# Frequency rows of a convolution stored with the channel block last, and the first MLP weights split earlier

## The chip, the cores and the metric

The kernel runs on one core of a Trainium2 chip. The metric is the device time of one execution in microseconds, median over runs; lower is better. PE is the matrix engine, ACT, DVE and POOL the scalar, vector and GpSimd engines, SP the engine that issues most transfers. `S.dma_start` issues a transfer from ACT, `nc.gpsimd.dma_start` from POOL.

## The reference

A block of 2048 tokens with 640 channels and adaptive layer norms, all in float32:

```
sa, ca, ga, sb, cb, gb = (silu(c) @ w_mod) in six parts of 640
h = layernorm(x) * (1 + ca) + sa
K = real(sum_n C_n B_n dt exp(dt A_n l)),  l = 0..2047          # a state-space kernel per channel
y = irfft(rfft(h, 4096) * rfft(K, 4096))[:2048] + h * Dskip     # long convolution along the tokens
x = x + ga * y
h = layernorm(x) * (1 + cb) + sb
x = x + gb * ((silu(h @ w1) * (h @ w3)) @ w2)                   # w1, w3: 640 x 1728
```

## The kernel before

**The convolution.** The transform is done as matrix products in two stages, of length `NA` = 32 and `NB` = 64. Channels are taken in `NDC` = 5 blocks of `DC` = 128. For each block there are eight groups `g` of four frequencies of the first stage: `stage2(ch, g)` transforms tokens and kernel, `k_copy` (ACT), `products` and `sums` (DVE) multiply them, `inverse1(ch, g)` does the first half of the inverse on PE into PSUM tile `pz`. `z_store` copies `pz` to SBUF tile `zt` on ACT and stores it in the scratch tensor `zs` in HBM: half a channel block (512 KB) at a time for blocks 0 to 3 from SP, and group by group (256 KB) from ACT for block 4 (`z_last`). Each group waits for three-deep buffers of the tables `s2` and `i1`, loaded by SP.

**The way back to tokens.** The second half of the inverse needs all frequencies of a token tile. Tile `j` holds 128 tokens (four values of `b`, 32 of `a`); `z_load(z, j, ks)` loads, for each channel block `k`, 64 partitions (cosine and sine parts of 32 frequencies) of four rows of 128 channels, 128 KB in all. In PE, `i2` turns this into tokens. There are 16 tiles. The first four (`early`, the first 512 tokens) are treated apart, in `x_part(j)`: blocks 0 to 3 come through memory like the others (loaded by POOL, block 3 just before it is used), but for block 4 the last two groups do not make the trip:

- Groups 0 to 5 (`NG` = 6, 24 frequencies) of block 4 are stored, and loaded again as soon as group 5 is stored, two gathers of 48 KB for each tile (cosine and sine rows apart): for tiles 0 to 2 from SP, for tile 3 from ACT. They land in `early[j][1]`, whose rest is zeroed by POOL beforehand. `far_cols` multiplies them with `i2`.
- Groups 6 and 7 are kept: `near_rows(g)` takes 32 columns of `i1` for the 16 values of `b` of the first four tiles, ACT copies the result to `near["z"]`, and `near_cols(g)` multiplies it with tables that `near_tables` built on POOL from the constant `i2d`. `far_cols` adds into the same PSUM tile `pl`.

For the last group, i = 7 of the loop that closes the convolution, PE's order is near_rows(7), `x_part(3)`, near_cols(7), far_cols, the ordinary inverse of group 7, three matmuls `fill`, and after them `keep_warm(IDLE)` with `IDLE` = 7 dummy matmuls. DVE adds `pl` to the 128 channels of each early tile (L1075), takes their statistics (L1078) and aggregates them (L1080).

**The first MLP.** `x_first` makes the power of variance on POOL, two tiles at a time, and normalises the tiles 0 and 2 on ACT and 1 and 3 on DVE. `turn_a` transposes them on PE, and `plain("A", 0, ...)`, the first block of the MLP's weights, begins. All weight products are made from two float32r parts: `split` copies a weight to its high part on ACT (`gh`, `uh`) and subtracts on DVE for the low part (`gl`, `ul`). For block 0 of `wg` and `wu` (`first_w`) the load is issued behind the last load of `i1`, and the split is ordered behind the last product sum of the convolution (`last_sum`). Loads of tiles 4 to 7, of weight block 13 and of weight block 1 follow on SP in the order in which they are written (`SQ`, `sp_order`).

The tile framework orders instructions of an engine by its own plan except where they are kept in program order (`tc.keep_in_program_order`, `ordered`, `acopy`, `act`) or placed behind another (`tc.issue_after`). Pools with `bufs=n` hand out the same n buffers in turn: `rw` (raw weights) has 5, `h` has 18.

Of the kernel before, what the change touches and what calls it, by code (L numbers as in the profile page):

```python
# [9 lines left out]
F32 = mybir.dt.float32  # L10
# [27 lines left out]
def consts():  # L38
# [25 lines left out]
    i2 = np.concatenate([np.cos(ang).T, -np.sin(ang).T] * 2)  # L64
# [17 lines left out]
    i1 = i1.reshape(*i1.shape[:-1], 2, NB).swapaxes(-1, -2).reshape(i1.shape)  # L82
    i2d = np.zeros((4, 16, 2, 2 * NA + 16))
    for fl in range(4):
        for c in range(2):
            for i in range(2):
                i2d[fl, :, c, i * NA:i * NA + NA] = i2[c * NA + (6 + i) * 4 + fl]
            i2d[fl, :, c, 2 * NA:] = np.eye(16)
    i2d = i2d.reshape(P, 2 * NA + 16)
# [27 lines left out]
def tile_kernel(ctx: ExitStack, tc: tile.TileContext, a):  # L117
# [5 lines left out]
    zs = dram.tile([NDC, NB, 2, NA, DC], F32, name="zs")  # L123
# [591 lines left out]
    def inverse1(ch, g):  # L715
# [5 lines left out]
        if ch == NDC - 1 and g >= NG:  # L721
            near_rows(g, i1, Y, pz[:, 0, 2 - 2 * (g % 2), :])
# [9 lines left out]
    near = {}  # L732
# [4 lines left out]
    def near_tables():  # L737

        hc = h_tile()[:, :2 * NA + 16]
        nc.sync.dma_start(hc, a["i2d"])  # L740
        for i in range(8 - NG):
            w = near["w", NG + i] = h_tile()
            G.tensor_tensor(w.rearrange("p (b a) -> p b a", b=16), bc(hc[:, 2 * NA:], 2, NA),
                            bc(hc[:, i * NA:i * NA + NA], 1, 16), op=OP.mult)
        near["z"] = h_tile()
        for x, z, st in early:
            G.memset(z[64:, :, 2 * DC:], 0.0)

    def near_rows(g, i1, Y, pd):
# [44 lines left out]
    def z_last(g):  # L794
# [4 lines left out]
        for j in (range(3), (3,), ())[g - NG + 1] if g >= NG - 1 else ():  # L799
            with tc.issue_after(stored.ins):  # L800
                for c in range(2):
                    r = slice(c * 32, c * 32 + 4 * NG)
                    ins = (S if j == 3 else nc.sync).dma_start(
                        early[j][1][64 + r.start:64 + r.stop, :, 2 * DC:], zsv[r, 4 * j:4 * j + 4, NDC - 1])
# [14 lines left out]
    def h_tile():  # L819
        return xp.tile([P, 512], F32, name="h", bufs=18)  # L820

    def z_tile():
        z = tz.tile([P, SD, 3, NA], F32, name="A")
        return z.rearrange("p k s b -> p (k s b)").rearrange("p (b d) -> p b d", b=4)

    ZW = (2 * DC, 3 * DC)
# [17 lines left out]
    def x_part(j, idle=0):  # L844
# [4 lines left out]
        for b in range(4):  # L849
            for hh in range(2):  # L850
                r, c = slice(hh * 64, hh * 64 + 64), slice(b * NA, b * NA + NA)
                ordered(py[hh][c, :2 * DC], i2[r], z[r, b, :2 * DC], start=True, stop=True,
# [159 lines left out]
    first_w = dict.fromkeys(("wg", "wu"))  # L1012
# [24 lines left out]
    for tk in range(NS - 4, LAG + 8 * NDC + 2):  # L1037
# [17 lines left out]
        if 0 <= i < 8:  # L1055
# [12 lines left out]
            if i == 7:  # L1068
# [3 lines left out]
                x_stats(3)  # L1072
                mv4 = xp.tile([P, 4, 2], F32, name="mv4", bufs=1)
# [37 lines left out]
    IDLE = 7  # L1111
# [21 lines left out]
    def z_place(both):  # L1133
        return wq.tile([P, 2, 2, 512], F32, name=both).rearrange("p a b c -> p (a b c)")[:, :4 * 3 * DC].rearrange(
            "p (b d) -> p b d", b=4)
# [8 lines left out]
    def x_first(tiles, mv):  # L1144
# [9 lines left out]
        for pair, rs in enumerate(powers):  # L1154
            V.scalar_tensor_tensor(rs[:, 2, :], mv[:, 2 * pair:2 * pair + 2, 0], -1.0, rs[:, 1, :],
                                   op0=OP.mult, op1=OP.mult)
            for i in range(2):
# [4 lines left out]
                else:  # L1162
                    V.tensor_scalar(xn, x, mv[:, j, 0:1], rs[:, 1, i:i + 1], op0=OP.subtract, op1=OP.mult)
# [11 lines left out]
    def x_mid(j, got, g):  # L1175
# [3 lines left out]
        for b in range(4):  # L1179
            for hh in range(2):  # L1180
                r, c = slice(hh * 64, hh * 64 + 64), slice(b * NA, b * NA + NA)
                n = ZW[hh]
                PE.matmul(py[hh][c, :n], i2[r], z[r, b, :n], start=True, stop=True, tile_position=(r.start, c.start))
        for hh in range(2):
            h = slice(hh * 256, hh * 256 + ZW[hh])
            V.tensor_tensor(x[:, h], py[hh][:, :ZW[hh]], x[:, h], op=OP.add)
# [97 lines left out]
    ahead = {(0, n): w for n, w in first_w.items()}  # L1284
# [15 lines left out]
    def wk(w, k):  # L1300
        return w[0][:, k, :], w[1][:, k, :]
# [7 lines left out]
    def plain(c, f, h, ws, early=False, between=None, then=None):  # L1309
# [6 lines left out]
        if early and f == 0:  # L1316
            pu = bank(1)
            for lo in range(2):
                for k in range(KD):
                    for ps, ws in ((pg, wgs), (pu, wus)):  # L1320
                        for i in range(1 if lo else 2):
                            end = PE.matmul(ps, ws[i][:, k, :], x[k][lo], start=(k + i + lo == 0),
# [267 lines left out]
    for pair in range(2):  # L1590
# [142 lines left out]
```

## Time and profile before

| | |
|---|---|
| median of 3 runs | 929.12 us (928.58 to 930.3) |
| the profiled execution | 927.25 us |
| its span, first to last instruction | 925.5 us |
| PE busy | 887.9 us, 96% |
| DVE, ACT, POOL busy | 698.9, 548.6, 265.9 us |
| convolution's last group to the MLP's first matmul | about 355 to 374 us |

In the profile's rows, `A<-zs` is a load of a `z` tile (its pool is named A), `zs<-zt` and `zs<-h` are the stores, `pl` is the PSUM tile of near and far columns, `py` that of x_part, `rw` a raw weight, `ps` any PSUM tile of the MLP part. L111 is the line of the helper through which all instructions of the MLP part go. A number in brackets is idle time before the instruction and what ended it. `PEclk` is the granted clock of PE, 1.00 throughout.

### The profile page before, as it was taken

The numbers are of one execution on the slowest core, as the hardware profiler recorded it, in microseconds if no ns is written. First come the engines' busy times: TensorE is split into PE (matmuls) and PEld (weight loads), VectorE is DVE, ScalarE is ACT, GpSimd is POOL, SyncE is SP. The second block draws the span as 40 slices with busy tenths as digits, with TensorE's granted clock in tenths as the row PEclk, the third lists the DMA queues.
The fourth block names the chain that finished last, engine by engine and source line by source line (L and its number), as shares of the span: only waits on it lengthen the run. The fifth ranks groups of instructions, "written<-read, shape, count | busy, mean of one in ns | idle before, by whom it ended". The sixth has DMA issues, their size and how long they took to land.

```text
span 925.5 us, 21047 instructions
## 1 busy us (share of the span) xinstructions
PE 887.9 (96%) x8461; PEld 692.2 (75%) x8461; DVE 698.9 (76%) x1250; ACT 548.6 (59%) x811; POOL 265.9 (29%) x278
## 2 busy tenths in 40 slices
PE   5999889999999998999999999999999999999998
PEld 3776567777777666678888887778888888888886
DVE  6799888999999967876666655686976666664665
ACT  4899899999999743564343323556633333333432
POOL 3633454445446330243222201210522222100000
PEclk9999999999999999999999999999999999999999
DMA  8755898655656887942131217974322211103452
GB/s 254 258 202 192 272 226 216 176 161 157 178 159 174 200 264 213 261 176 86 57 111 60 58 44 217 278 234 153 95 64 71 85 58 57 58 29 100 150 177 101
DMA packets 103765, 140.68 MB, mean 152 GB/s; under 512 B 20212, under 2 KB 62964, under 8 KB 103668
## 3 DMA queue, kind: packets, MB, share of 16 engines
q1 hardware_dynamic: 100108, 129.48, 46.9%
q0 software_dynamic: 2048, 7.34, 2.4%
q10 hardware_dynamic: 1512, 2.52, 0.8%
q8 instruction: 66, 1.08, 0.5%
q14 instruction: 31, 0.25, 0.1%
HBM read 107.85 MB, written 31.46 MB: 151 GB/s over the span
## 4 chain that ended last, share of the span: by engine, by line
PE 67%; ACT 14%; DVE 12%; DMA 4%; issue 2%; SPq 0%; POOL 0%; DVEq 0%; ACTq 0%; POOLq 0%
PE ps L111 58%; ACT A L145 3%; PE p L676 3%; ACT ph L145 2%; ACT cs L145 2%; DVE E L597 2%; ACT L145 2%; DVE uk L111 2%; PE pm L111 1%; DVE A L604 1%; ACT kc L148 1%; PE pt L637 1%; DVE E L600 1%; ACT uk L148 1%; DMA A<-zs 1%
## 5 line engine op out<-in xcount | busy, mean ns | idle before, releaser
L111 DVE TENSOR_TENSOR s<-ps,s 128x512 f32<-128x512 f32 x138 | 95.0, 688 | 80.1 <-PE ps L111 79.8
L570 POOL TENSOR_TENSOR ph<-thi,iota 128x1024 int32<-128x1024 int32 x40 | 86.0, 2150 | 142.3 <-DVE A L608 94.9
L111 DVE TENSOR_TENSOR gl<-rw,gh 128x640 fp32r<-128x640 f32 x87 | 78.1, 897 | 64.3 <-ACT gh L111 64.3
L111 ACT CAST gh<-rw 128x640 fp32r<-128x640 f32 x87 | 63.2, 727 | 100.4 <-PE ps L111 62.6
L111 PE MATMUL ps<-xA,gh 128*128 128x512 f32 x280 | 88.5, 393 | 0.1
L111 PE MATMUL ps<-gh,uh 128*128 128x512 f32 x224 | 87.5, 390 | 0.0
L111 PE MATMUL ps<-gl,uh 128*128 128x512 f32 x224 | 87.2, 389 | 0.0
L111 POOL TENSOR_TENSOR S<-rw 128x256 f32<-128x256 f32 x46 | 36.5, 795 | 174.1 <-DVE S0l L111 163.1
L676 PE MATMUL p<-uk,s 128*64 128x256 f32 x640 | 77.9, 385 | 6.8 <-DVE Y L701 2.4
L111 PE MATMUL ps<-gh,ul 128*128 128x512 f32 x208 | 81.1, 390 | 0.0
L676 PEld LDWEIGHTS p<-uk,s 128*64 128x64 f32 x640 | 44.6, 136 | 29.5 <-DVE Y L701 3.5
L111 PEld LDWEIGHTS ps<-xA,gh 128*128 128x128 f32 x280 | 52.2, 188 | 13.6 <-issue 1.0
L111 PE MATMUL ps<-xA,gl 128*128 128x512 f32 x140 | 54.5, 390 | 0.0
L604 DVE TENSOR_TENSOR A<-A,ph 128x1024 f32<-128x1024 f32 x40 | 51.8, 1295 | 0.0
L111 ACT ACTIVATE s<-ps 128x512 f32<-128x512 f32 (+1 forms) x33 | 19.7, 597 | 53.1 <-PE ps L111 53.1
L597 DVE TENSOR_TENSOR E<-A,cs 128x1024 f32<-128x1024 f32 x40 | 50.2, 1254 | 0.6 <-ACT A L145 0.6
L111 PEld LDWEIGHTS ps<-gl,uh 128*128 128x128 f32 x224 | 42.1, 188 | 9.0
L111 PEld LDWEIGHTS ps<-gh,uh 128*128 128x128 f32 x224 | 42.1, 188 | 8.8
L111 PEld LDWEIGHTS ps<-gh,ul 128*128 128x128 f32 x208 | 39.0, 188 | 8.4
L574 POOL TENSOR_TENSOR ph<-ph,phi 128x512 int32<-128x512 int32 x40 | 44.5, 1115 | 2.5
L727 PE MATMUL pz<-Y,i 64*128 64x128 f32 x640 | 44.4, 278 | 0.7 <-ACT h L148 0.4
L727 PEld LDWEIGHTS pz<-Y,i 64*128 64x128 f32 x640 | 38.9, 187 | 7.1 <-issue 5.8
(251 smaller groups left out, 2287.8 us busy)
## 6 DMA issues: line engine op xcount, KB each, us to landing
rw<-in_w_dram SPq DMA_DIRECT2D x52, 320.0 KB, 2.9
us<-u SPq DMA_DIRECT2D x16, 640.0 KB, 3.2
s<-in_s_dram SPq DMA_DIRECT2D x40, 256.0 KB, 4.8
i<-in_i_dram SPq DMA_DIRECT2D x40, 256.0 KB, 3.3
rw<-in_wg_dram SPq DMA_DIRECT2D x31, 320.0 KB, 3.9
rw<-in_wu_dram SPq DMA_DIRECT2D x28, 320.0 KB, 2.8
uk<-us SPq DMA_DIRECT2D x32, 256.0 KB, 4.6
zs<-zt SPq DMA_DIRECT2D x16, 512.0 KB, 4.8
```

Of the source, the lines that this page charges most:

```text
L111: ins = fn(*args, **kw)
L145: return tc.keep_in_program_order(S.activation(*args, **kw))
L148: return tc.keep_in_program_order(S.copy(out, in_))
L570: keep(G.tensor_tensor(p, bc(thi[:, s * SD:s * SD + SD], 2, NPH), bc(iota, 1, SD), op=OP.mult))
L574: keep(G.tensor_tensor(p[:, :, :NA], p[:, :, :NA], bc(phi[:, s * SD:s * SD + SD], 2, NA), op=OP.add))
L597: keep(V.tensor_tensor(EC[s][:, :, 1:3, :], AA[s][:, :, 1:3, :], mid(cs[s]), op=OP.mult))
L600: keep(V.tensor_tensor(EC[s][:, :, 0, :], AA[s][:, :, 0, :], cs[s][:, :, 2 * NA - 1:NA - 1:-1], op=OP.mult))
L604: keep(V.tensor_tensor(A[:, :, 1:3, :], A[:, :, 1:3, :], mid(ph[s]), op=OP.mult))
L637: keep(PE.matmul(pt[c * 64:c * 64 + 64, g, :], kk[:, g, :], s1[:, c, :], start=True, stop=True, tile_position=(0, c * 64)))
L676: keep(PE.matmul(p2[par * 64:par * 64 + 64, pi, c, :], s2[:, pi * 2 + par, c * 64:c * 64 + 64], uk[:, 0:kn + 1:kn, f, :], start=True, stop ...
L727: ins = keep(PE.matmul(pz[:, par, (g % 2) * 2 + pi, :], i1[r, pi, c, :], Y[r, pi, c, :], start=(c == 0), stop=(c == 1), tile_position=(par ...
```

## The change

- `zs` is laid out with the channel block slowest, then frequency, cosine or sine, `b`, channel. A load of one tile and block has four rows of 128 channels in one piece: 64 rows of 2 KB where there were 256 of 512 B. A store has for each partition four or eight pieces of 512 B where there was one of 2 or 4 KB. Tables `i1` and `i2` are reordered to fit, and `z` tiles hold the channel block first.
- For `far_cols`, cosine and sine rows are now neighbours: one gather of 48 rows for each early tile, all four from SP behind the store of group 5. `far_cols` uses those 48 partitions alone; the zeroing on POOL goes. `near_rows` takes its 32 columns from the constant `i2d`, which grows from 80 to 336 columns.
- The loads of the first weights are written inside `near_rows(7)`, still behind the last `i1`. Their high parts are copied on ACT right after x_part(3)'s copy, into further `rw` buffers, and the low parts made on DVE (`first_low`): that of `wg` ahead of the sums of `pl`, that of `wu` after `x_first`. A low part is two instructions, for k = 0 to 3 and for k = 4, into `h` tiles.
- `x_first`'s DVE instructions are kept in program order. `IDLE` is 5. Loads of tiles 6 and 7 are issued ahead of those of weight block 1.

```diff
-    zs = dram.tile([NDC, NB, 2, NA, DC], F32, name="zs")
+    zs = dram.tile([NDC, NA, 2, NB, DC], F32, name="zs")
...
+    def first_low(w, hi, lo, lo4):
+        for out, k in ((lo, slice(4)), (lo4, 4)):
+            tc.keep_in_program_order(V.tensor_tensor(out, w[:, k], hi[:, k].bitcast(F32), op=OP.subtract))
...
         near["z"] = h_tile()
-        for x, z, st in early:
-            G.memset(z[64:, :, 2 * DC:], 0.0)
...
-                    ordered(pd[fl * 32:fl * 32 + 32], i1[r, pi, c, :32], Y[r, pi, c, :],
+                    ordered(pd[fl * 32:fl * 32 + 32], near["i1"][r, (g - NG) * 2 + pi, c], Y[r, pi, c, :],
                             start=(c == 0), stop=(c == 1), tile_position=(par * 64, fl * 32))
         acopy(near["z"][:, (g - NG) * P:(g - NG) * P + P], pd)
         if g == 7:
+            raw = [xp.tile([P, KD, P], F32, name="rw", bufs=5) for _ in range(2)]
+            for w, name in zip(raw, ("wg", "wu")):
+                with tc.issue_after(i1_last[0].ins):
+                    w_get(w, 0, name)
             x_part(3)
+            rest_lo = h_tile(F32R)
+            for i, w in enumerate(raw):
+                hi = xp.tile([P, KD, P], F32R, name="rw", bufs=5)
+                acopy(hi, w)
+                lo = h_tile(F32R).rearrange("p (k c) -> p k c", k=4)
+                first_w.append((w, hi, lo, rest_lo[:, i * P:i * P + P]))
             near_cols(7)
             far_cols()
...
+    far = slice(64, 64 + 8 * NG)
...
-                ordered(near["pl"][b * NA:b * NA + NA, j * P:j * P + P], i2[64:], z[64:, b, 2 * DC:], start=False, stop=True,
+                ordered(near["pl"][b * NA:b * NA + NA, j * P:j * P + P], i2[far], z[far, 2, b], start=False, stop=True,
...
-    zst = [zs[k].rearrange("b c f d -> (b c) f d") for k in range(NDC)]
-    zsv = zs.rearrange("k b c f d -> (c f) b k d")
+    zst = [zs[k].rearrange("f c b d -> (c b) f d") for k in range(NDC)]
+    zsv = zs.rearrange("k f c b d -> k (f c) b d")
...
         stored = S.dma_start(zst[NDC - 1][:, g * 4:g * 4 + 4], zt)
-        for j in (range(3), (3,), ())[g - NG + 1] if g >= NG - 1 else ():
+        for j in range(4) if g == NG - 1 else ():
             with tc.issue_after(stored.ins):
-                for c in range(2):
-                    r = slice(c * 32, c * 32 + 4 * NG)
-                    ins = (S if j == 3 else nc.sync).dma_start(
-                        early[j][1][64 + r.start:64 + r.stop, :, 2 * DC:], zsv[r, 4 * j:4 * j + 4, NDC - 1])
-                    if j < 3:
-                        zlast[0] = ins
+                zlast[0] = nc.sync.dma_start(early[j][1][far, 2], zsv[NDC - 1, :8 * NG, 4 * j:4 * j + 4])
...
-            q.dma_start(z[hh * 64:hh * 64 + 64, :, kk * DC:kk * DC + DC], zsv[:, 4 * j:4 * j + 4, k])
+            q.dma_start(z[hh * 64:hh * 64 + 64, kk], zsv[k, :, 4 * j:4 * j + 4])
...
                 x_stats(3)
+                first_low(*first_w[0])
...
-    for name in first_w:
-        first_w[name] = xp.tile([P, KD, P], F32, name="rw", bufs=5)
-        with tc.issue_after(i1_last[0].ins):
-            w_get(first_w[name], 0, name)
...
-    IDLE = 7
+    IDLE = 5
...
-            V.scalar_tensor_tensor(rs[:, 2, :], mv[:, 2 * pair:2 * pair + 2, 0], -1.0, rs[:, 1, :],
-                                   op0=OP.mult, op1=OP.mult)
+            tc.keep_in_program_order(V.scalar_tensor_tensor(rs[:, 2, :], mv[:, 2 * pair:2 * pair + 2, 0], -1.0, rs[:, 1, :],
+                                                            op0=OP.mult, op1=OP.mult))
...
-                    V.tensor_scalar(xn, x, mv[:, j, 0:1], rs[:, 1, i:i + 1], op0=OP.subtract, op1=OP.mult)
+                    tc.keep_in_program_order(V.tensor_scalar(xn, x, mv[:, j, 0:1], rs[:, 1, i:i + 1],
+                                                             op0=OP.subtract, op1=OP.mult))
...
-        ws = first_plain.pop() if first_plain else plain_weights(simple[0], last_sum)
+        ws = first_plain.pop() if first_plain else [
+            ([hi[:, k] for k in range(KD)], [lo[:, k] for k in range(4)] + [lo4]) for _, hi, lo, lo4 in first_w]
...
             x_first(tiles, mv4)
+            first_low(*first_w[1])
...
+            got += [x_get(6, x_place("T40")), x_get(7, x_place("T30"))]
             fetch(1, "wg")
             fetch(1, "wu")
-            got += [x_get(6, x_place("T40")), x_get(7, x_place("T30"))]
```

More of the change, by code (lines that the diff above doesn't have):

```diff
@@ L721, in inverse1 @@
         if ch == NDC - 1 and g >= NG:
-            near_rows(g, i1, Y, pz[:, 0, 2 - 2 * (g % 2), :])
+            near_rows(g, Y, pz[:, 0, 2 - 2 * (g % 2), :])
         for pi in range(2):
@@ L731, in tile_kernel @@
     NG = 6
-    near = {}
+    near, first_w = {}, []
+    def first_low(w, hi, lo, lo4):
+        for out, k in ((lo, slice(4)), (lo4, 4)):
+            tc.keep_in_program_order(V.tensor_tensor(out, w[:, k], hi[:, k].bitcast(F32), op=OP.subtract))
     def ordered(*args, **kw):
@@ L737, in near_tables @@
     def near_tables():
-        hc = h_tile()[:, :2 * NA + 16]
+        hc = h_tile()[:, :2 * NA + 16 + 8 * NA]
+        near["i1"] = hc[:, 2 * NA + 16:].rearrange("p (g c b) -> p g c b", g=4, c=2)
         nc.sync.dma_start(hc, a["i2d"])
@@ L851, in x_part @@
                 r, c = slice(hh * 64, hh * 64 + 64), slice(b * NA, b * NA + NA)
-                ordered(py[hh][c, :2 * DC], i2[r], z[r, b, :2 * DC], start=True, stop=True,
+                ordered(py[hh][c, :2 * DC], i2[r], z[r, :2, b], start=True, stop=True,
                         tile_position=(r.start, c.start))
@@ L1181, in x_mid @@
                 r, c = slice(hh * 64, hh * 64 + 64), slice(b * NA, b * NA + NA)
-                n = ZW[hh]
-                PE.matmul(py[hh][c, :n], i2[r], z[r, b, :n], start=True, stop=True, tile_position=(r.start, c.start))
+                n = ZK[hh] * DC
+                PE.matmul(py[hh][c, :n], i2[r], z[r, :ZK[hh], b], start=True, stop=True, tile_position=(r.start, c.start))
         for hh in range(2):
-            h = slice(hh * 256, hh * 256 + ZW[hh])
-            V.tensor_tensor(x[:, h], py[hh][:, :ZW[hh]], x[:, h], op=OP.add)
+            n = ZK[hh] * DC
+            h = slice(hh * 256, hh * 256 + n)
+            V.tensor_tensor(x[:, h], py[hh][:, :n], x[:, h], op=OP.add)
         power[0] = G.dma_start(xs[j], x)
@@ L1282, in tile_kernel @@
     loaded = [None]
-    ahead = {(0, n): w for n, w in first_w.items()}
+    ahead = {}
     def fetch(f, name):
@@ L1321, in plain @@
                         for i in range(1 if lo else 2):
-                            end = PE.matmul(ps, ws[i][:, k, :], x[k][lo], start=(k + i + lo == 0),
+                            end = PE.matmul(ps, wk(ws, k)[i], x[k][lo], start=(k + i + lo == 0),
                                             stop=(lo == 1 and k == KD - 1))
```

25 lines of the change are left out of this document (13 added, 12 removed).

## The prediction

> **What bounds the kernel now.** I read the page first, for the share of each engine, then busy time by stretch, then the chain of waits from 330 to 412 us, then the timelines of ACT, PE and DVE in the few microseconds where that chain leaves PE.
>
> ```profile
> span 925.5 us, 21047 instructions
> PE 887.9 (96%) x8461; PEld 692.2 (75%) x8461; DVE 698.9 (76%) x1250; ACT 548.6 (59%) x811; POOL 265.9 (29%) x278
> ```
>
> ```profile
> core 0: us, PE busy (x) PEld busy (x) DVE busy (x) ACT busy (x) POOL busy (x), PEclk, DMA share, GB/s
> ...
> 363.00:367.80 4.80, 2.98 (x54) 1.80 (x44) 1.53 (x6) 0.46 (x2) 0.00 (x0) 1.00 0.85 241
> 367.80:372.90 5.10, 4.68 (x37) 3.58 (x37) 4.30 (x17) 3.58 (x5) 1.96 (x4) 1.00 0.87 226
> 372.90:377.40 4.50, 4.41 (x26) 3.55 (x26) 4.19 (x7) 4.03 (x7) 0.00 (x0) 1.00 0.83 241
> 377.40:408.50 31.10, 30.43 (x187) 22.28 (x188) 23.64 (x47) 17.90 (x28) 10.76 (x18) 1.00 0.90 258
> 408.50:925.00 516.50, 512.27 (x2371) 416.71 (x2371) 342.31 (x583) 212.87 (x375) 94.02 (x122) 1.00 0.34 106
> ```
>
> PE is the bound, 96% of the span. From 372.90 on it hardly stops: whatever lets the MLP begin earlier there is carried to the end one for one, and what the change does to the many later loads of z is hidden. The stretch 363.00 to 367.80 stands out: PE has 2.98 us of work in 4.80, and ACT and DVE are idle too. In 367.80 to 372.90 PE is filled with dummy matmuls while it waits for a chain of small operations.
>
> ```profile
> 337.51 3.80 DMA zs<-zt
> ...
> 341.92 4.48 DMA A<-zs
> ...
> 346.44 0.66 PE py L735 x14
> ...
> 357.26 4.45 DMA zs<-h
> ...
> 363.87 3.04 DMA A<-zs
> ...
> 367.04 0.73 PE pl L735 x16
> ...
> 367.80 0.49 DVE xm L1075 x2
> ...
> 369.38 0.72 POOL rs L111
> ...
> 370.85 0.85 POOL rs L111
> ...
> 371.92 0.93 ACT T L111
> ...
> 377.39 22.94 PE ps L111 x133
> ```
>
> The chain names the two round trips through memory that the change touches. The store of the last half of channel block 3 (337.51) releases the gather of the block for tile 0 (341.92), on which PE waits at 346.44. The store of group 5 (357.26) releases the gathers for the far columns (the last issued at 363.87, landed 366.91), and after them come columns, statistics, power, normalised tile and MLP.
>
> **The far columns: eight gathers become four, all on SP's queue.**
>
> ```profile
> 362.40 1.49 ACTq L803 DMA_DIRECT2D A<-zs  x2
> 363.94 0.27 ACT L148 COPY h<-pz 128x128 f32<-128x128 f32 x1 [2.08 <-DMA zs<-h]
> 364.10 0.30 ACT L148 COPY xm<-xe 128x128 f32<-128x128 f32 x1
> ```
>
> ```profile
> 362.70 0.62 PE L735 MATMUL py<-A,i 64*32 64x256 f32 x12
> 364.35 1.13 PE L735 MATMUL pl<-h 128*128 128x128 f32 x8 [1.02 <-ACT h L148]
> 365.41 0.42 PE L735 MATMUL pl<-A,i 64*32 64x128 f32 x8
> 366.15 0.42 PE L735 MATMUL pl<-A,i 64*32 64x128 f32 x8 [0.32 <-DMA A<-zs]
> ```
>
> ```profile
> L803 SPq DMA_DIRECT2D A<-zs x6: 322/370/407, 361.8 to 363.9; - x6
> ```
>
> ```profile
> DMA to landing us min/median/max: 2.3/4.0/6.6
> ```
>
> Before, ACT issues tile 3's two gathers itself (362.40 to 363.89), and the copy of near_rows(7) queues behind them; PE, done with x_part(3) at 363.32, waits 1.02 us for it. Gone from ACT, the copy can start when its operand is ready, about 362.95, and near_cols(7) at 363.35 instead of 364.35. It takes 1.06 until the far columns begin at 365.41: now 364.4.
>
> SP issues six gathers from 361.77 at about 0.4 us; it will issue four, the last near 363.0. Its landing was 3.04 us behind the issue; at that, 366.0. The second row is that of ACT's eight stores of the last block, rows of 2 KB, 2.3 us at best. The new gather has such rows and a quarter of the packets for its bytes, so I take 2.4 and 365.4. The far columns take 32 PE instructions, 0.32 us for eight when nothing is missing, 1.3 us in all: 364.4 + 1.3 = 365.7, and tile 3's quarter is needed at 365.4. They ended at 367.74. Gain 2.0 us, by bounds 1.3 (landing 366.0, then a quarter of the columns) to 2.0.
>
> **The first weights.** Both hi copies go to ACT behind the copy of xe, both lo parts to DVE, the first ahead of the sums of the far columns, the second behind the four normalisations.
>
> ```profile
> 364.10 0.86 DVE L863 BATCH_NORM_STATS2 st<-xm 128x6 f32<-128x128 f32 x4
> ...
> 370.12 0.16 DVE L111 SCALAR_TENSOR_TENSOR rs<-mv,rs 128x2 f32<-128x2 f32 x1 [0.18 <-POOL rs L111]
> 370.20 0.28 DVE L1080 BATCH_NORM_AGGREGATE mv<-st 128x2 f32<-128x30 f32 x1
> ...
> 372.32 0.82 DVE L111 TENSOR_TENSOR gl<-rw,gh 128x640 fp32r<-128x640 f32 x1
> ```
>
> ```profile
> 369.37 0.73 ACT L111 CAST gh<-rw 128x640 fp32r<-128x640 f32 x1
> ```
>
> ```profile
> 370.56 0.20 POOL L111 TENSOR_TENSOR rs<-mv,epst 128x2 f32<-128x2 f32 x1 [0.47 <-DVE mv L1080]
> ```
>
> Two casts of 0.73 run on ACT from about 363.5 to 365.0, where it is idle. DVE ends its statistics of tile 3 at 364.96 and adds the first lo part, 0.82 in one piece and now in two: free at 365.8. So the sums start at 365.85 rather than 367.80: the cover of this step is just used up, and if the far columns came earlier still, DVE would be late next. The second lo part starts after the last normalisation, ends about 5.1 us after the sums start, and PE needs it some 6 us after. The casts that leave 369.37 to 370.72 free only the first ACT tile, which the chain does not go through: nothing.
>
> What does count is the written order. Before, DVE took the bias of pair 0 (370.12), waiting 0.18 for POOL, ahead of the last aggregate (370.20), on which POOL waits 0.47 for the second pair's power, which the chain goes through. Held in order, the aggregate ends about 0.35 earlier, and POOL, free of pair 0 at 370.09, starts the second pair about 0.3 us earlier. I take 0.35; bounds 0 (the scheduler does it otherwise) and 0.47.
>
> **The stores in 512-byte rows.** Sixteen stores of 512 KB go from rows of 4 KB to eight rows of 512 B each, and the eight last ones from 2 KB. The trace has no store of 512 B; the nearest rows are loads of 512 B (first), stores of 4 KB (second) and ACT's stores of 2 KB (third), of three windows.
>
> ```profile
> q1 hardware_dynamic: 717, 0.35, 80.9%
> ```
>
> ```profile
> q1 hardware_dynamic: 88, 0.35, 99.4%
> ```
>
> ```profile
> q10 hardware_dynamic: 576, 1.05, 22.0%
> ```
>
> The windows are 372.0 to 373.5, 146.1 to 147.0 and 342 to 355. Engine time per MB: 0.809 x 16 x 1.5 / 0.35 = 55 us; 0.994 x 16 x 0.9 / 0.35 = 41 us; 0.22 x 16 x 13 / 1.05 = 44 us. A 512 KB store thus takes 0.524 x (55 - 41) / 16 = 0.5 us longer, a 256 KB one 0.2. In the convolution rounds nobody waits for that: no wait there names a load of tables or channels. On the chain, the store of 337.51 lands 0.5 later; the gather for tile 0 behind it now has a quarter of the rows, for 128 KB 0.131 x (55 - 44) / 16 = 0.1 us less, and shares the engines with smaller packets: I take 0.3 later for PE at 346.44, and this moves all that follows. Bounds: -0.5 (PE's wait before x_part(0) goes) and +1.5 (a store costing twice the load's rate: 0.524 x (110 - 41) / 16 = 2.3, less the slack). The store of group 5 takes 0.2 longer, which the 0.3 between tile 3's landing and its use covers.
>
> [...]
>
> **The rest.** Four memsets leave POOL, which is busy for 29% of the span. The constants' load grows from 40 to 168 KB, 0.3 us at these rates, and is read at 359. Two dummy matmuls less: PE waits for ACT's tile behind them, nothing. The loads of weight block 1 move behind twelve transfers:
>
> ```profile
> 374.83 0.60 SPq L111 DMA_DIRECT2D rw<-in_wg_dram  x1
> ```
>
> ```profile
> 387.58 0.50 PE L111 MATMUL ps<-xA,gh 128*128 128x512 f32 x1
> ```
>
> Block 1 is first used at 387.58, then 385.5. Twenty-seven issues of 0.4 to 0.6 us from 363.4 put the load at 374 to 380, landing 3.9 later; cast and lo part take 1.55. So 379.5 to 385.4, just in time: nothing, at most 0.5 late.
>
> **Sum.** -2.0 - 0.35 + 0.3 = -2.05 us. The profiled execution took 927.25 us, its span 925.5 with 1.75 around it; it would take 925.2. The median of the three runs shown is 929.12, 1.87 above the profiled one, so I state 929.12 - 2.05 = 927.1.
>
> **Rivals.** *More than that (0.13).* The gathers of tile 0 come early enough to end PE's 0.56 us wait at 346.44, and the wait below goes because tiles 6 and 7 are in sooner: 2.35 + 0.56 + 0.68 = 3.6 us, 925.5 us. Against it: this wait is for DVE's splits, not for data.
>
> ```profile
> 408.50 0.50 PE L111 MATMUL ps<-xB,gh 128*128 128x512 f32 x1 [0.68 <-DVE xB L111]
> ```
>
> *The wait moves to the stores (0.22).* Group 5's store was already the slow one (4.45 us against 2.3 for the next) because one engine's queue was behind; with four times the packets it lands 1.5 later, and 0.3 of that is covered: gain 2.05 - 1.2 = 0.85, 928.3 us, no measurable change.
>
> *Slower (0.13).* Writes of 512 B cost more than reads. At a rate r the half-block store delays PE by 0.524 (r - 41) / 16 - 0.2 and group 5's by 0.262 (r - 44) / 16 - 0.3. Together they eat the 2.35 at r = 100 us per MB, nearly twice the load's rate, and are 1.86 beyond it at 137; at r = 170 they are 4.0 and 1.8, and the kernel is 3.4 us slower, 932.5. For it: no such row exists in the trace; against it: loads and stores of equal rows cost the same here (41 and 44 for stores of 4 and 2 KB).
>
> *Block 1 late (0.05).* At the 241 GB/s of 372.90 to 377.40 the 1.97 MB ahead of it take 8.2 us, PE waits some 3 us at 385.5: 930.1 us.
>
> **Numbers.** The forecast has 0.47. A measurement of this kernel tells about 0.2%, 1.86 us, from no change, and the forecast lies just beyond; of its 0.47 I count 0.36 as faster. With 0.13 and 0.02 of the store rival: faster 0.51. Same: 0.11, the store rival's other 0.20, 0.02 of the slow one and 0.04 of block 1: 0.37. Slower: 0.11 and 0.01. The forecast's own range is 926.2 to 928.2; the stated one, 924.9 to 930.5, takes in the first two rivals and block 1 and leaves out about 0.15.
>
> **What would show it.** Right: no gather on ACT's queue; near_rows(7)'s copy within 0.2 us of its matmuls; far columns without a wait for A; the second power of POOL 3.5 us after the first sum, against 3.9; the first MLP matmul at 372.2 instead of 374.29, and the stretch from there to the end as long as before. Wrong: PE waiting over 1 us at x_part(0), group 5's store taking over 6 us, or a PE wait near 385 for the block 1 split.

## The result and the profile after

The changed kernel takes 936.97 us in the median of six runs (934.08 to 940.38), the kernel before, in the same session, 930.33 us (928.58 to 931.44): 1.0069 times as long, with an interval of 1.0043 to 1.0095. That is 6.6 us slower where 2.05 us faster was forecast, and outside the stated range of 924.9 to 930.5.

The head of the page of the changed kernel:

```profile
span 938.6 us, 21033 instructions
PE 892.5 (95%) x8459; PEld 696.1 (74%) x8459; DVE 699.1 (74%) x1252; ACT 548.8 (58%) x811; POOL 262.0 (28%) x274
```

The span is 13.1 us longer than the 925.5 before, PE's busy time only 4.6: most of the rest is PE waiting. About half of the 13.1 is spread between executions: the one profiled here (940.38 us) is the slowest of its six, the one of before (927.25) faster than all its six. Two marks on PE's timeline cut the span: the first matmul of the MLP, and the first matmul on the second half of the tokens (`xB`). The kernel before:

```profile
374.29 0.48 PE L111 MATMUL ps<-xA,gh 128*128 128x512 f32 x1
...
405.39 0.62 PE L111 MATMUL ps<-xB,gh 128*128 128x512 f32 x2
```

The changed kernel (the bracket is idle time before the instruction and what ended it):

```profile
379.58 0.47 PE L111 MATMUL ps<-xA,rw 128*128 128x512 f32 x1
...
400.73 1.22 PE L111 MATMUL ps<-xA,gh 128*128 128x512 f32 x2 [7.05 <-ACT gh L111]
...
418.28 0.62 PE L111 MATMUL ps<-xB,gh 128*128 128x512 f32 x2
```

The MLP begins 5.3 us later, its first half lasts 38.70 us instead of 31.10, 7.6 longer, and from the second mark to the end it is 520.3 against 520.1. So next to nothing is lost after 418 us. In the first half one wait stands out, 7.05 us before block 1's gate weights: the sign that the prediction had named last. Busy time by stretch (PEclk is the granted clock of PE):

```profile
core 0: us, PE busy (x) PEld busy (x) DVE busy (x) ACT busy (x) POOL busy (x), PEclk, DMA share, GB/s
349.00:353.20 4.20, 4.18 (x32) 1.97 (x32) 1.53 (x6) 0.00 (x0) 0.00 (x0) 0.59 0.66 169
371.50:379.60 8.10, 7.97 (x72) 6.46 (x72) 4.68 (x19) 3.37 (x5) 1.79 (x4) 0.79 0.57 170
...
395.00:400.70 5.70, 0.00 (x0) 0.00 (x0) 4.66 (x12) 1.69 (x4) 2.15 (x5) 0.70 0.43 172
400.70:404.70 4.00, 3.97 (x11) 3.13 (x12) 3.11 (x6) 2.77 (x4) 3.04 (x6) 0.58 0.90 293
```

The wait costs twice: after it PE runs for 4 us at a clock of 0.58, where the profiled execution of before had 1.00 throughout. The same shows in small at 349 and 371.5, behind waits for data of 2.42 and 2.44 us. What the long wait waits for is in the chain of waits of the changed kernel, which no longer goes through the statistics, but through SP:

```profile
371.52 1.19 PE pl L739 x24
372.71 1.42 PE pz L727 x16
...
374.77 3.36 DMA zs<-h
...
378.15 0.44 SPq L111
...
388.58 5.24 DMA rw<-in_wu_dram
...
398.95 0.17 DVE nb L111
...
399.14 0.03 ACT T L111
...
399.97 0.72 ACT gh L111
```

The last of SP's first eight loads of tiles 4 and 5 stands until group 7's store has landed (374.77 + 3.36 = 378.13); then SP issues the loads written ahead of block 1's at about 0.6 us each, and reaches block 1 at 388.10, where it had been at 374.83. The gate weights land 4.9 us later, at 393.0, the up weights at 393.82, and still the copy on ACT starts only at 399.97: ACT's planned order has the normalisation of tile 6 ahead of it, which waits for what DVE makes of the tile's statistics (`nb`):

```profile
399.14 0.92 ACT L111 ACTIVATE T<-T,nb,rs 128x640 f32<-128x640 f32 x1 [4.01 <-DVE nb L111]
```

### The profile page after: what moved, and what is told of

The parts are those of the page before. It is cut to its first block, busy times and chain, and to the rows that moved or that the text cites. A ratio compares the mean times of both kernels' runs of the same rounds, so it can differ in the third digit from the quotient of the medians.

```text
span 938.6 us, 21033 instructions
## 1 busy us (share of the span) xinstructions
PE 892.5 (95%) x8459; PEld 696.1 (74%) x8459; DVE 699.1 (74%) x1252; ACT 548.8 (58%) x811; POOL 262.0 (28%) x274
## 4 chain that ended last, share of the span: by engine, by line
PE 69%; ACT 12%; DVE 10%; DMA 5%; issue 2%; SPq 1%; POOL 0%; DVEq 0%; ACTq 0%; POOLq 0%
PE ps L111 55%; PE p L676 4%; ACT A L145 3%; ACT ph L145 2%; DVE E L597 2%; ACT cs L145 2%; PE pz L727 2%; PE pm L111 2%; ACT L145 2%; PE pt L637 1%; PE pu L111 1%; DMA A<-zs 1%; DVE uk L111 1%; PE pa L111 1%; SPq L111 1%
## 5 line engine op out<-in xcount | busy, mean ns | idle before, releaser
L111 PE MATMUL ps<-xA,gh 128*128 128x512 f32 x270 | 84.8, 395 | 7.1 <-ACT gh L111 7.1
L676 PE MATMUL p<-uk,s 128*64 128x256 f32 x640 | 79.4, 391 | 7.1 <-DVE Y L701 2.3
L676 PEld LDWEIGHTS p<-uk,s 128*64 128x64 f32 x640 | 45.3, 139 | 30.6 <-issue 4.2
```

What stands on the lines that cost most here:

```text
L111: ins = fn(*args, **kw)
L676: keep(PE.matmul(p2[par * 64:par * 64 + 64, pi, c, :], s2[:, pi * 2 + par, c * 64:c * 64 + 64], uk[:, 0:kn + 1:kn, f, :], start=True, stop ...
```

## The experiments

The reading above leaves three suspects: the moved loads, the new layout with its 512-byte stores, and the early first weights. Four kernels take them apart: one undoes the moved loads, three make one part alone.

**The order of loads undone.** The changed kernel, with block 1 fetched ahead of tiles 6 and 7 again.

```diff
-            got += [x_get(6, x_place("T40")), x_get(7, x_place("T30"))]
             fetch(1, "wg")
             fetch(1, "wu")
+            got += [x_get(6, x_place("T40")), x_get(7, x_place("T30"))]
```

> The changed kernel, with the loads of weight block 1 ahead of those of tiles 6 and 7 again, as before. Theory A (three separate losses: the order of loads 7 us, a late x_part(0) with a slow PE clock behind it 3.5 us, late far gathers 2 to 3 us): PE's wait of 7.05 us for the block 1 cast goes, and the time falls by about 7 us, to 929 to 932 us. Rival B (the 512-byte stores make everything late, and block 1 with it): the wait stays at 4 us or more and the time falls by less than 3 us, to 934 or more.

Measured: 927.47 us, ratio to the kernel before 0.9961 (0.994 to 0.9982). One move of two lines turns 6.6 us lost into a gain of 3.6, more than theory A expected. SP's and ACT's timelines in this kernel:

```profile
374.90 0.51 SPq L111 DMA_DIRECT2D rw<-in_wg_dram  x1
375.53 0.36 SPq L111 DMA_DIRECT2D rw<-in_wu_dram  x1
```

```profile
381.77 0.72 ACT L111 CAST gh<-rw 128x640 fp32r<-128x640 f32 x1
382.38 0.73 ACT L111 CAST uh<-rw 128x640 fp32r<-128x640 f32 x1
```

From the start of the MLP (373.93 here) block 1's copy is 7.8 us away, in the changed kernel 20.4, and the only PE wait from 372 us to the end is the old one:

```profile
PE ps L111 <- DVE xB L111: 0.7, 1, 0.7
```

**Layout and gathers alone**, on the kernel before: the line below and what follows from it, the loads, the tables and the gathers of the far columns. (The channel block is slowest and the channels are last in both layouts; frequency and `b` change places.)

```diff
-    zs = dram.tile([NDC, NB, 2, NA, DC], F32, name="zs")
+    zs = dram.tile([NDC, NA, 2, NB, DC], F32, name="zs")
...
```

> The kernel before with the new layout of zs alone (stores in pieces of 512 B, loads of 2 KB rows, one far gather a tile, all four on SP); weights, DVE order, dummy matmuls and order of loads as before. Theories A and B alike: PE waits 2 us or more at x_part(0), the granted clock falls behind it, the last far gather lands 4 to 5 us after its issue; 4 to 6 us slower than before, 933 to 936 us. Rival C (those waits hang on where an instruction fetch falls): PE waits under 1 us at one of the two places, and the time is within 2 us of before.

Measured: 928.5 us, 0.998 (0.996 to 1.0001). The loss that the trace of the changed kernel had suggested to me before 380 us does not exist by itself: theories A and B missed. PE waits 1.71 us before x_part(0) and 0.25 and 0.77 us at the far columns, and its clock stays at 1.00 behind them.

**Early first weights alone**, on the kernel before, with their loads and copies in near_rows(7), x_first in written order and `IDLE` = 5.

```diff
+                first_low(*first_w[0])
...
```

> The kernel before with the first weights split early, DVE's written order and 5 dummy matmuls; layout and order of loads as before. Theory A: the power of the second pair starts 0.3 to 0.4 us sooner after the sums, 0.3 to 0.5 us faster, not to be told from before (929 to 931 us). Rival: the lo part ahead of the sums or the shorter row of dummy matmuls costs something: 1 us or more slower.

Measured: 929.25 us, 0.9985 (0.9962 to 1.0008). It is not a loss either; alone, neither half can be told from no change.

**The order of loads alone**, on the kernel before.

```diff
+            got += [x_get(6, x_place("T40")), x_get(7, x_place("T30"))]
             fetch(1, "wg")
             fetch(1, "wu")
-            got += [x_get(6, x_place("T40")), x_get(7, x_place("T30"))]
```

> The kernel before with only the order of loads changed: tiles 6 and 7 ahead of weight block 1. Theory A: block 1 is issued near 388 us and cast behind tile 5's norm, PE waits 3 to 6 us for it, and the time is 3 to 6 us longer, 933 to 936 us. Rival B: without the late stores the order costs under 1 us, 929 to 931 us.

Measured: 937.07 us, 1.0063 (1.003 to 1.0096). The swap is slow without anything else, by a little more than theory A's 933 to 936. PE's waits from 372 us on in this kernel:

```profile
PE ps L111 <- DVE gl L111: 2.7, 1, 2.7
PE ps L111 <- ACT gh L111: 2.1, 1, 2.1
```

So the moved loads are the cause. Next: is it that they land late, or that ACT's and DVE's planned orders put the weights behind the tiles?

**Copies first.** The changed kernel, loads in its order, with block 1's copies held ahead of tile 6's normalisation on ACT.

```diff
+            held[0] = pair == 0 and n == 1
             if n < len(simple) - 1:
-                ws = None
+                ws = plain_weights(simple[2]) if held[0] else None
...
+            if held[0]:
+                tc.keep_in_program_order(cast)
...
+        if held[0]:
+            tc.keep_in_program_order(norm)
```

> The changed kernel; loads in its order, but on ACT the copies that round block 1's gate and up weights are put ahead of tile 6's norm. Theory P (the loads landed at 393 and 394 us; what made PE wait 7 us is that ACT's planned order has the norm of tile 6, which waits 4 us for DVE, ahead of the two copies): the copies begin when the loads land, PE's wait for the gate weights falls from 7.1 us to at most 3 us, time 931 to 933.5 us (the changed kernel had 937.0). Theory L (the loads themselves are late, the copies' place is nothing): PE's wait stays over 5.5 us, time 935.5 us or more. A third way, that the wait only moves to DVE's low part of the weights (behind tile 7's statistics): a PE wait of 3 to 6 us that ends on DVE's operation, 933.5 to 936.

Measured: 934.66 us, 1.0046 (1.0019 to 1.0072): the third way. PE's timeline, then DVE's:

```profile
390.19 0.73 PE L111 MATMUL ps<-xA,gh 128*128 128x512 f32 x2 [2.12 <-ACT gh L111]
395.68 0.80 PE L111 MATMUL ps<-xA,gl 128*128 128x512 f32 x1 [4.75 <-DVE gl L111]
...
412.75 0.62 PE L111 MATMUL ps<-xB,gh 128*128 128x512 f32 x2
```

```profile
394.01 0.89 DVE L111 BATCH_NORM_STATS2 st<-T 128x6 f32<-128x320 f32 x2
394.81 0.81 DVE L111 TENSOR_TENSOR gl<-rw,gh 128x640 fp32r<-128x640 f32 x1
```

The one wait of 7 us has become two of 2.1 and 4.8, the second for the low part, which DVE's own plan has behind the statistics of tile 7. The first half (MLP begins at 374.00) lasts 38.75 us, as in the changed kernel's first profile: nothing was won in it.

**Copies and low parts first.** The same, with DVE's low parts of block 1 ahead of the additions of tiles 6 and 7.

```diff
+            if held[0]:
+                tc.keep_in_program_order(low)
...
+            if held[0]:
+                tc.keep_in_program_order(add)
```

> As the run with block 1's copies first on ACT (934.7 us, PE waits 2.1 us for the gate weights' rounded copy and then 4.8 us for their low part), with, on DVE too, the low parts of block 1's gate and up weights ahead of the additions and statistics of tiles 6 and 7; loads still in the changed order. Theory P (the place of the copies and low parts in the planned orders of ACT and DVE is the cost, the later loads alone are little): the second wait goes, 2 to 3 us of the first stay, and with them part of PE's slow clock; time 929 to 931.5 us. Theory L (the loads' landing itself costs): the second wait shrinks but the time stays at 932.5 us or more. Third way: the norms of tiles 6 and 7 come later by the 1.6 us of the low parts and PE waits for them at the second half's transposes: 931.5 to 934 with a PE wait on ACT's norm.

Measured: 932.53 us, 1.0013 (0.9994 to 1.0032), outside theory P's range and at the edge of theory L's. It lies in the third way's range too, but PE's wait for a norm is 0.23 us here, not its price. The second wait is gone, and the first half lasts 34.50 us (375.19 to 409.69). Timeline and stretches of PE:

```profile
391.41 0.81 PE L111 MATMUL ps<-xA,gh 128*128 128x512 f32 x2 [2.14 <-ACT gh L111]
```

```profile
389.20:391.40 2.20, 0.07 (x4) 0.00 (x0) 0.73 (x3) 2.04 (x3) 0.00 (x0) 1.00 0.86 250
391.40:395.40 4.00, 3.95 (x10) 2.79 (x11) 3.29 (x7) 2.08 (x3) 0.38 (x1) 0.57 0.98 362
395.40:409.70 14.30, 14.07 (x73) 11.64 (x72) 8.57 (x19) 8.73 (x14) 6.77 (x11) 1.00 0.72 248
```

Of the 7.6 us between the profiles, 4.2 were the two planned orders. The other 3.4 are what later loads cost even then: 2.1 of waiting and 4.0 x 0.43 = 1.7 of slow clock, of which the rest of the half gives 0.4 back. The medians divide the loss about evenly: by the ratios, 4.0 to 5.2 us between the changed kernel and this one, 4.8 to 5.5 from here to the order undone.

**Block 1 between tiles 6 and 7.**

```diff
-            got += [x_get(6, x_place("T40")), x_get(7, x_place("T30"))]
+            got += [x_get(6, x_place("T40"))]
             fetch(1, "wg")
             fetch(1, "wu")
+            got += [x_get(7, x_place("T30"))]
```

> The changed kernel with block 1's two loads between the loads of tile 6 and those of tile 7, so behind six transfers and not twelve. Theory P: ACT's order then has the copies ahead of tile 6's norm, and the loads are issued about 6 x 0.6 = 3.6 us earlier; PE's wait falls from 7.1 us to under 2 us, time 928 to 931.5 us. Theory L: the time falls by the earlier issue alone, 3.6 us at most, 933.5 to 935 us. If neither place matters (what e1 undid was something else, such as which loads share the queues with the far gathers): 936 us or more.

Measured: 932.58 us, 1.0025 (0.9997 to 1.0054), a miss of both theories by a little. PE waits 2.77 us instead of 7.05, yet in the profile the first half is no shorter, 38.66 us (374.48 to 413.14), because the clock stays low for 10 us:

```profile
387.90:390.70 2.80, 0.03 (x2) 0.02 (x1) 0.81 (x2) 2.09 (x4) 0.48 (x1) 1.00 1.02 397
390.70:401.20 10.50, 10.50 (x34) 5.88 (x35) 6.09 (x15) 2.09 (x3) 3.03 (x7) 0.52 0.58 192
```

10.5 x 0.48 = 5.0 us of slow clock behind a wait of 2.8.

**The wait filled.** The changed kernel, with 24 matmuls on a zero tile where PE waits; their sums are overwritten. The matmuls of tile 7 are held in order ahead of them.

```diff
+        if early and f == 1:
+            for _ in range(24):
+                tc.keep_in_program_order(PE.matmul(pg, idle[:, :P], idle, start=True, stop=True))
```

> The changed kernel, with 24 matmuls on a zero tile on PE (about 5.5 us at the full clock) in the place where it waits 7.1 us for block 1's gate weights; their sums are overwritten. If PE's slow clock after the wait (granted 0.70 and 0.58 in the two stretches of the profile) comes of its idling: the granted clock behind the wait is 0.9 or more, and the time falls by about 4.0 x 0.42 = 1.7 us, to 934.5 to 936 us (937.0 before). If the slow clock comes of something else (the wait's length is all that counts): 936.5 to 938 us. If the filling matmuls disturb DVE or ACT, or last beyond the wait: over 938 us.

Measured: 935.03 us, 1.0039 (1.0019 to 1.0058). PE's timeline and stretches:

```profile
388.06 5.78 PE L111 MATMUL ps<-idle 128*128 128x512 f32 x24
395.19 0.73 PE L111 MATMUL ps<-xA,gh 128*128 128x512 f32 x2 [1.36 <-ACT gh L111]
```

```profile
395.00:399.00 4.00, 3.68 (x15) 2.78 (x16) 3.27 (x6) 2.95 (x5) 3.21 (x6) 1.00 0.90 277
```

Filling and waiting together are as long as the wait was, 5.78 + 1.36 = 7.1 us, but the clock behind them is 1.00, and the first half lasts 37.53 us (374.05 to 411.58), 1.2 less. In this execution, then, the slow clock behind the wait came of PE standing idle, and was about a sixth of the loss in the first half. The medians alone do not tell this kernel from the changed one: 1.0039 has an interval that overlaps those of 1.0056 and 1.0069.

**The cost of 512-byte stores.** The kernel before, its rows in memory spaced so that stores write pieces of 512 B and loads stay as they were.

```diff
-    zs = dram.tile([NDC, NB, 2, NA, DC], F32, name="zs")
+    zs = dram.tile([NDC, NB, 2, NA, DC + 32], F32, name="zs")[:, :, :, :, :DC]
```

> The kernel before, with only the rows of the frequency buffer in memory set 32 numbers further apart, so that each store writes pieces of 512 bytes while the loads still read 512-byte rows. Theory S (small store rows are slow, the forecast's dearest rival): the 512 KB store takes 4 us or more longer, tile 0's inverse waits for it, 932 us or more. Theory N (a 512-byte packet costs about as much per byte as a larger one): the store before tile 0's inverse lands at most 0.5 us later, time within 1 us of the kernel before.

Measured: 929.53 us, 0.9991 (0.9967 to 1.0014). The small pieces cost nothing that can be measured in the time; the rival *Slower* (932.5 us) is refuted. The stores do land later, 5.2 us after the issue in the median against 4.8 in the kernel before. This run's profile, the slowest of its ten executions (932.99 us), begins the MLP as late as the changed kernel's first, at 379.84, with none of the change in it but the spaced rows.

**The early tiles one group later**, on the kernel with the order undone.

```diff
-            if i in (2, 3, 5):
-                x_part((0, 0, 0, 1, 0, 2)[i])
+            if i in (3, 4, 5):
+                x_part(i - 3)
```

> The changed kernel with the loads of block 1 back ahead of tiles 6 and 7 (927.5 us by an earlier run), and the first three early tiles' inverse one group later on PE: tile 0 after group 3, tile 1 after group 4, tile 2 after group 5, so that tile 0's does not wait for the last of its rows. If that wait (1.1 us in the earlier run of the undone order, 2.4 us and a drop of PE's clock in the changed kernel) is on the path: the wait goes and the time falls by 0.7 to 1.5 us, 926 to 926.8. If the far columns or the DVE's sums set the end instead, the wait turns up there: 927 to 928. If tile 2's inverse after group 5 delays the near rows: 928 to 930.

Measured: 927.62 us, 0.9973 (0.9942 to 1.0003), no gain over 927.47. The wait before x_part(0) goes, and a wait turns up at the far columns, as the second expectation had it:

```profile
368.29 0.42 PE L739 MATMUL pl<-A,i 48*32 48x128 f32 x8 [2.61 <-DMA A<-zs]
```

**Both kernels once more**, the changed one and the one with the order undone, in one session.

> The changed kernel once more, unaltered, to see whether the 5.3 us by which its profile begins the MLP late (379.6 us, where runs with the same code up to there began at 373.9 to 375.2) belong to the change. Theory E (they belong to that one execution: the landing of the gathers differs from run to run by microseconds): the MLP begins at 373.5 to 376.5 us, the stretch from there to the first matmul of the second token half is 38.7 us again against 31.1 us before, and the median is 31.1 + 7.5 later than with the order undone, 934 to 936.5 us. Theory F (they belong to the change): the MLP begins at 378 us or later, and the time is 938 us or more.

> The changed kernel with block 1's loads back ahead of those of tiles 6 and 7, beside the changed kernel in the same session. If the swap is the loss and the rest a gain: 927 to 928.5 us, a ratio to the kernel before of 0.995 to 0.998, and 7.5 us below the changed kernel. If the 927.5 us of its first run were luck of the early part: 929.5 to 931.5 us, no change from before.

Measured: 937.32 us, 1.0056 (1.0032 to 1.0079), and 927.67 us, 0.9954 (0.9932 to 0.9975). The second version beats both kernels, twice, and the two medians are 9.65 us apart, where 7.5 was expected. The wait in the changed kernel:

```profile
397.69 1.22 PE L111 MATMUL ps<-xA,gh 128*128 128x512 f32 x2 [7.05 <-ACT gh L111]
```

With nearly equal starts (376.56 and 376.21), the first half lasts 39.56 us with the swap and 31.21 without; 8.4 of the 9.1 us between the two spans (935.9 and 926.8) lie there. The wait is 7.05 us as before. Theory E's bounds are missed by a little (376.56 for 376.5, 39.56 for 38.7, 937.3 for 936.5), theory F's start of 378 by more: at least 3 of the 5.3 us by which the MLP began late in the first profile belonged to that execution.

The two marks over the executions profiled (first half is from the first MLP matmul to the first on `xB`):

| kernel | MLP begins | first half | median |
|---|---|---|---|
| before | 374.29 | 31.10 | 930.33 to 931.49 |
| changed | 379.58, 376.56 | 38.70, 39.56 | 936.97, 937.32 |
| order undone | 373.93, 376.21 | 31.18, 31.21 | 927.47, 927.67 |
| layout and gathers alone | 376.06 | 31.12 | 928.5 |
| early first weights alone | 375.78 | 31.18 | 929.25 |
| early tiles later | 375.66 | 31.20 | 927.62 |
| 512-byte stores, on before | 379.84 | 31.13 | 929.53 |
| order alone, on before | 375.97 | 36.45 | 937.07 |
| copies first | 374.00 | 38.75 | 934.66 |
| copies and low parts first | 375.19 | 34.50 | 932.53 |
| between tiles 6 and 7 | 374.48 | 38.66 | 932.58 |
| wait filled | 374.05 | 37.53 | 935.03 |

With block 1's loads early, every kernel has 31.1 to 31.2 us in the first half; with them late, none is below 34.5.

## Why the prediction was wrong

**The step that failed: "The loads of weight block 1 move behind twelve transfers ... just in time: nothing, at most 0.5 late".** It cost 9.65 us in the medians of one session (937.32 - 927.67). Three things were missing from it.

First the issue time, forecast as 374 to 380 us. The working counted issues at 0.4 to 0.6 us and left out what SP waits for between them. SP's timeline of the changed kernel:

```profile
369.15 9.45 SPq L111 DMA_DIRECT2D A<-zs  x8
...
384.36 3.00 SPq L111 DMA_DIRECT2D A<-zs  x5
...
388.10 0.36 SPq L111 DMA_DIRECT2D rw<-in_wg_dram  x1
388.58 0.36 SPq L111 DMA_DIRECT2D rw<-in_wu_dram  x1
```

Eight issues that would take 5 us take 9.45, 3.0 of them in the wait for group 7's store; fifteen more at 0.6 follow, and 388 came of it. But that wait does not decide: in the second profile it is 0.3 us, block 1 is issued at 385.09, and PE waits 7.05 us as before. Over the six profiles with this order the issue lies between 382.58 and 388.10. The kernel before had the pace: from the end of its far gathers (361.77 + 2.47 = 364.24) to block 1 (374.83) SP needs 10.6 us for thirteen issues, waits included, 0.8 each. Twenty-five of the forecast's twenty-seven issues stand ahead of block 1; at that pace, from its 363.4, they end at about 384. In the kernel before block 1 stood only three issues behind the eight and had time to spare until 387.58.

Second the copy. "Cast and lo part take 1.55" was added to the landing, as if ACT and DVE served block 1 when it came. They work in a planned order, and the written order of the loads is an input to that plan: with the loads behind tiles 6 and 7, so were copy and low part. The profiles give this 4.2 of the 7.6 us, the medians about half of the loss.

Third the clock, which the prediction left at 1.00: 1.2 us by the filled wait, 4.0 x 0.42 = 1.7 by the changed kernel's own clock.

The rival *Block 1 late* had the right place, 5 chances in 100, and a price of 3 us, from bytes ahead at the rate of the engines. The run with copies and low parts first has 3.4 us for later loads alone, but the nearness is luck: 1.7 of it is slow clock, and most of the lateness came of SP's issues, not of bytes: the load was issued at 384.88 there, against 380 at the latest in the forecast. The planned order, which the rival did not count, was at least as much again.

**Far columns, -2.0.** The queue was right: no gather is on ACT, and near_rows(7)'s copy waits for PE alone. In the changed kernel:

```profile
367.19 0.27 ACT L148 COPY h<-pz 128x128 f32<-128x128 f32 x1 [1.13 <-PE pz L739]
```

The landing was not sure: 2.4 us behind the issue were taken, and in the changed kernel's first profile the second of the four gathers took 4.89, with PE waiting 2.44. In the runs with the order undone PE waits 0 and 0.40 there, so the size is the execution's. The first of them has the far columns as the prediction saw them, without a wait:

```profile
366.77 1.08 PE L739 MATMUL pl<-A,i 48*32 48x128 f32 x32
```

To free the term of where the step begins, count from PE's start on group 6's ordinary inverse (360.06 before) to the end of the far columns: 7.68 us before (7.74 to 9.59 in the three other profiles with the old gathers), forecast 5.64. In nine profiles with the new gathers and the early tiles in their old place it is 5.47 in three, 6.36 to 7.30 in five and 8.44 in the changed kernel's first profile. The gain of 2.0 is there when the gathers land in time; in the middle one of the nine it is 0.9.

**DVE's written order, -0.35.** Right in kind and size: the second power follows the first directly, 1.07 us from start to start (374.36, 375.43) against 1.47 before (369.38, 370.85).

```profile
374.36 0.71 POOL L111 TENSOR_TENSOR rs<-rs,epst 128x2 f32<-128x2 f32 x1
...
375.43 0.69 POOL L111 TENSOR_TENSOR rs<-rs,epst 128x2 f32<-128x2 f32 x1
```

**Stores, +0.3.** Roughly borne out for the store: the one ahead of tile 0's gather, forecast 0.5 us longer, took 4.1 to 4.5 us in the ten profiles with the new layout (4.35 in the middle), against 3.80, 3.91 and 4.15 in three with the old. From middle to middle (4.35 and 3.91) that is 0.44 us, near the 0.5 forecast from the rows, though the two ranges touch. In the whole kernel it cannot be seen: the spaced rows moved the time by less than 0.35% either way. Group 5's store took 4.71 us in the changed kernel's first profile against 4.45, not the 1.5 later of the rival *The wait moves to the stores*; its reason, that one engine's queue was behind, fits the profile of before, where from 359.80 to 361.20 us the mean DMA share is 0.06, one of the sixteen engines. That loads and stores of equal rows cost the same was argued there from two figures of stores alone; in the changed kernel ACT's eight stores, in pieces of 512 B, took 0.177 x 16 x 40 / 2.10 = 54 us of engine time per MB (q10, 2.10 MB and 17.7% of 340 to 380 us), beside the 55 of the loads of 512 B before.

**The sum of the rest.** Without the swap the change gains 3.6 and 3.8 us in the two sessions, with intervals of about 1.7 to 5.6 and 2.3 to 6.3; the forecast of 2.05 lies in the first, and just outside the second. The first MLP matmul at 372.2 was never seen; 373.93 was the earliest. One reason is the execution I worked from: at 927.25 us it was as fast as any of the kernel before (927.26 to 935.44 in the first session of experiments), so its early waits were short already. Group 6's inverse, from which the steps above are counted, begins at 360.06 there, but at 362.38 and 363.83 with the order undone. From it to the first MLP matmul it is 14.23 us before, and 11.55 and 12.38 with the order undone: 2.7 and 1.9 us gained, about the 2.35 forecast for this stretch, and hidden in these profiles by the later start. Whether the start is late by the change or by the execution stays open: two profiles of kernels with the old layout have 361.15 and 361.68. How the 3.6 divide between far columns, layout and DVE's order stays open: the parts alone gave 0.998 and 0.9985, each with an interval that takes in 1. Why the gathers land at such different times from one execution to the next stays open too.

## What to carry to other kernels

A load that is moved back in a queue has to be followed to the end: what the issuing engine waits for before it gets there, when it lands, and then where the planner has put the instructions that consume it, because the plan moves with the load. A wait of the bound engine near a moved step deserves its full price, wait and slow clock (here 7.05 us and 1.2 to 1.7), before it is called "just in time". When a change of several parts loses, undoing the suspected part from the whole and making each part alone finds the culprit; here it took four kernels, and left a version faster than both.

## What was not expected of the hardware

A wait of 2.1 us (copies and low parts first) or 2.8 us (between tiles 6 and 7) was followed by a granted clock of 0.57 for 4.0 us and of 0.52 for 10.5 us; waits of 1.36 us (the filled wait) and 1.02 us (before) by 1.00. The length of the wait alone does not decide: 1.71 us before x_part(0) (layout and gathers alone) left the clock at 1.00, while behind 1.60 us at the same place (order undone, second run) the next sixteen matmuls (L676) took 3.13 us, elsewhere in that profile 1.95. In the changed kernel, taken from where the clock changes to where it changes back:

```profile
349.40:352.80 3.40, 3.40 (x30) 1.72 (x16) 1.53 (x6) 0.00 (x0) 0.00 (x0) 0.51 0.69 180
...
373.30:376.70 3.40, 3.30 (x18) 2.70 (x15) 3.09 (x14) 1.85 (x3) 1.79 (x4) 0.51 0.72 205
...
397.20:404.10 6.90, 3.37 (x8) 2.67 (x9) 5.79 (x14) 4.33 (x6) 5.19 (x10) 0.51 0.56 183
```

The granted clock is then 0.51, and it stays so for 3.4 us, or 6.8, or (between tiles 6 and 7, from 391.0 to 401.3) 10.2. All slow stretches between 340 and 430 us in the fourteen profiles have one of these three lengths, and the starts within one execution lie whole multiples of 3.41 us apart: 373.3 and 397.2 are seven such steps behind 349.4 and 373.3. In these profiles, then, the clock changes on a beat of 3.41 us, and waits of one length can cost different amounts: in the changed kernel's second profile the same wait of 7.05 us brings 10.2 us of slow clock, 392.6 to 402.9, of which 5.2 lie behind it, against 3.4 in the first. The kernel before is not free of slow stretches either: the mean clock of its executions in the sessions above lies between 0.984 and 1.000.

How much idle time in a step is enough, and why the clock stays low for three steps with PE busy all through (between tiles 6 and 7, 10.50 us of 10.50), stays open.

A z load of 64 rows of 2 KB takes SP about as long to issue as one of 256 rows of 512 B: 3.00 us for five in the changed kernel, 0.60 each, against 0.64 before:

```profile
376.08 3.22 SPq L111 DMA_DIRECT2D A<-zs  x5
```

Thus the new layout bought next to nothing on SP's queue, on which the moved loads stood.
